# A branch for the general case: eight batches written out, or a loop over the batches with dynamic addresses

## The chip, the cores and the metric

One Trainium2 chip, one core of it. The metric is the device time in microseconds (us), the median of the runs of one program. The kernel before takes 548.6 us (three runs, 548.52 to 548.7).

## The reference

Eight batches of eight heads, 1024 positions of width 64. Keys and values are projected along the sequence to 64 rows (E and F), then comes softmax attention, and its output, laid out as 8192 tokens of width 512, goes through a gated feed-forward block of width 1536.

```python
k_proj = einsum('ks,bhsd->bhkd', E, k)
v_proj = einsum('ks,bhsd->bhkd', F, v)
scores = scale * matmul(q, k_proj.transpose(0, 1, 3, 2))
attn = exp(scores - max(scores))
attn = attn / (sum(attn) + 1e-09)
x = matmul(attn, v_proj)          # then (batch, seq, heads * width), 8192 x 512
g, val = x @ w_gate, x @ w_val
out = (g * sigmoid(g) * val) @ w_out
```

## The kernel before

The work is cut into 16 chunks `c` of 512 tokens, two to a batch, and each chunk into 12 slices `f` of the feed-forward width. The program has two halves.

**The main path** (lines 797 to 977) is one region written out by hand: `tc.manual_schedule()` keeps the instructions of each engine in the order in which they are written. A loop in Python over 192 steps (lines 966 to 975) emits `f_g` and `f_v`, eight matmuls of 128x512 with the tanh on ScalarE and two products on VectorE. Between them `run_slot` drops the attention of the next batches into numbered slots, and `late` gives the second matrix product of the chunk before (`f_m`: seven half-size products in place of eight, with sums on VectorE and GpSimd). Loads go out on GpSimd's queue, results on SyncE's. `f_m_last` (lines 671 to 710) ends the last chunk; its six last transfers of 128 KB go out from lines 695 and 706.

The main path takes the exponential without subtracting the row's maximum. Therefore it adds up the sums of the exponentials (`u_Z`, `u_sum`) and makes a flag from them (`u_flag`): 0 if the sum is sane, 1 if not. `u_bad` (lines 763 to 765) loads the flag into a register of each of the five engines and marks a place for a branch hint there, in slot 88 after 48 x 6 (the flag is loaded at 518.8 to 522.7 us of the span).

**The general path** (`general`, lines 767 to 795) is the other half. It stands behind `with tc.If(bad[0] != 0, label="general")` (line 979) and computes all again, with the maximum subtracted (`exp_maxed`, line 374: eight exponentials in place of one). In Python it is `for b in range(B)`: each of the eight batches is written out with constant addresses. An engine whose flag is 0 branches over all of it, to the code after the `If`, where the program ends: SyncE waits for every output transfer and every engine, a barrier of all engines follows, the semaphores are cleared, and a second barrier closes (in the trace these have line 1006, the branch and its arm line 979). The inputs of the measurement give a flag of 0: no instruction of `exp_maxed` stands in the trace.

The two halves share their helpers: `load_k`, `load_v`, `load_q`, `u_N`, `rows_of` and so on are called by both, and `maxed` tells them that it is the general path that is being emitted.

Of the kernel before, what the change touches and what calls it, by code (L numbers as in the profile page):

```python
# [15 lines left out]
B = 8  # L16
H = 8
S = 1024
# [5 lines left out]
NJ = S // P  # L24
# [3 lines left out]
CH = 2  # L28
# [11 lines left out]
def kernel(  # L40
# [55 lines left out]

    kb, vb, qb, xT, hT = {}, {}, {}, {}, {}

    def load_k(b, h0=0, h1=H):
        if b or maxed:  # L100
            kb[b] = kv_pool.tile([P, H, NJ, D], BF16, name="kb", tag="kb")
        nc.gpsimd.dma_start(
            out=kb[b][:, h0:h1].rearrange("p h j d -> p h (j d)"),
            in_=k[b, h0:h1].rearrange("h (p j) d -> p h (j d)", j=NJ),
        )

    def load_v(b, heads=(0, H)):
        if heads[0] == 0:
            vb[b] = kv_pool.tile([P, H, NJ, D], BF16, name="vb", tag="vb")
        t = vb[b]  # L110
        for h0, h1 in zip(heads, heads[1:]):
            nc.gpsimd.dma_start(  # L112
                out=t[:, h0:h1].rearrange("p h j d -> p h (j d)"),
                in_=v[b, h0:h1].rearrange("h (p j) d -> p h (j d)", j=NJ),
            )

    def load_q(b, ch, js=(0, 4), hs=(0, H)):
        if js[0] == 0 and hs[0] == 0:
            qb[b, ch] = q_pool.tile([P, H, 4, D], BF16, name="qb", tag="qb")
        js, hs = slice(*js), slice(*hs)  # L120
        nc.gpsimd.dma_start(  # L121
            out=qb[b, ch][:, hs, js, :].rearrange("p h j d -> p h (j d)"),
            in_=q[b, hs].rearrange("h (p c j) d -> p c h j d", c=2, j=4)[:, ch, :, js, :].rearrange(
                "p h j d -> p h (j d)"
            ),
        )
# [16 lines left out]
    maxed = []  # L143
# [14 lines left out]
    def u_KV(b, what="kv", hs=(0, H), at="a"):  # L158

        key = (b, what)  # L160
        if key not in kvp:
            kvp[key] = bank(at, [P, H, D], FP32, "kvp")
        t = kvp[key]
        h0, h1 = hs
        todo = [x for x in (("k", 0, ET, kb), ("v", 64, FT, vb)) if x[0] in what]
        for j in range(NJ):
            for _, lo, w, src in todo:
                nc.tensor.matmul(  # L168
                    out=t[lo : lo + 64, h0:h1].rearrange("p h d -> p (h d)"),
                    lhsT=w[:, j, :],  # L170
                    rhs=src[b][:, h0:h1, j, :],
                    start=(j == 0),
                    stop=(j == NJ - 1),
                )
        if "k" in what:
            nc.scalar.copy(out=ks[b % 2][0:64, h0:h1], in_=t[0:64, h0:h1])
        if "v" in what:
            tv = t[64:128].rearrange("p (g r e) d -> p g r e d", r=2, e=2)
            for r in range(2):
                vs = VS[b % 2][64 * r : 64 * r + 64].rearrange("p (g e) d -> p g e d", e=2)  # L180
                nc.vector.tensor_copy(out=vs, in_=tv[:, :, r])
        if h1 == H:
            kvp.pop(key)
# [76 lines left out]
    def u_KT(b, at="a", prs=(0, NPAIR)):  # L260

        t = bank(at, [P, NPAIR, KP], FP32, "kTp")
        for pr in range(*prs) if b > 1 or maxed else ():
            nc.tensor.matmul(
                out=t[:, pr, :],
                lhsT=ks[b % 2][:, 2 * pr : 2 * pr + 2, :].rearrange("p h d -> p (h d)"),
                rhs=ident_bf[:, 0:KP],  # L270
                start=True,
                stop=True,
            )
        for g in range(2) if b < 2 and not maxed else ():
            turn_ksp(t, b, g)
        bd = BD[b % 2][:].rearrange("p (a c) k -> p a c k", c=2)
        for c in range(2):
            src = t[64 * c : 64 * c + 64, slice(*prs)]
            nc.vector.tensor_copy(out=bd[0:64, slice(*prs), c, 0:64], in_=src)
            nc.vector.tensor_copy(out=bd[64:128, slice(*prs), c, 64:128], in_=src)  # L280
# [31 lines left out]
    def first_batch(kind, shape, name):  # L312

        n, ms = kept[kind]
        kept[kind] = (n + 1, ms)
        return hs_tile(ms[n % len(ms)], shape, name)

    def u_T(b, u, at="a", eng=nc.scalar):
        ch, w = divmod(u, 4)
        g, i = divmod(w, 2)  # L320
        ps = bank(at, [P, 4, P], BF16, "qTp")
        src = qb[b, ch]
        for n in range(4):
            nc.tensor.transpose(  # L324
                out=ps[:, n, :],
                in_=src[:, 4 * g + n, 2 * i : 2 * i + 2, :].rearrange("p j d -> p (j d)"),
                identity=ident_bf[:],
            )
        t = first_batch("q", [P, 4, P], "qT")
        copy(eng, t[:], ps[:])  # L330
        qT[b, u] = t
# [17 lines left out]
    def u_S(b, u, at="a"):  # L349
        ch, w = divmod(u, 4)  # L350
        g, i = divmod(w, 2)
        ps = bank(at, [P, 4, P], FP32, "sc")
        if (b, ch) in by_dma:
            t = qT[b, ch, "d"][:].rearrange("p (h i) t -> p i h t", i=2)[:, i, 4 * g : 4 * g + 4]
        else:
            t = qT.pop((b, u))
        for n in range(4):
            slot = (0, 2, 1, 3)[n] if (b, ch) in by_dma or maxed else n
            nc.tensor.matmul(  # L359
                out=ps[:, slot, :], lhsT=t[:, n, :], rhs=BD[b % 2][:, 4 * g + n, :], start=True, stop=True  # L360
            )
        e = aw.tile([P, 4, 2, KP], FP32, name="ee", tag="ee", bufs=4)
        ee[b, u] = e
        if maxed:
            exp_maxed(e, ps)
            return
        nc.scalar.activation(  # L367
            out=e[:].rearrange("p h j k -> p (h j k)"),
            in_=ps[:].rearrange("p a k -> p (a k)"),
            func=AF.Exp,  # L370
            scale=scale,
        )
# [20 lines left out]
    def u_N(b, u, eng=nc.gpsimd):  # L393
        ch, w = divmod(u, 4)
        g, i = divmod(w, 2)
        if (b, ch) in by_dma:
            if (b, ch, "d") not in AA:
                AA[b, ch, "d"] = aw.tile([P, 4, H, KP], BF16, name="AAd", tag="AAd")
            a = AA[b, ch, "d"][:, 2 * i : 2 * i + 2, 4 * g : 4 * g + 4, :]
        else:  # L400
            a = AA[b, u] = first_batch("a", [P, 2, 4, KP], "AA")
            a = a[:]
        zr, r = rr.pop((b, u))
        eng.tensor_tensor(  # L404
            out=a.rearrange("p j h k -> p h j k"),
            in0=ee.pop((b, u))[:],
            in1=r.unsqueeze(3).to_broadcast([P, 4, 2, KP]),
            op=ALU.mult,
        )
        unwatched.append(zr)  # L410
        if b or u > 3 or maxed:
            u_Z()

    unwatched = []
# [1 line left out]
    def u_Z():  # L416
        for zr in unwatched:
            nc.gpsimd.tensor_tensor(out=zsum[:], in0=zsum[:], in1=zr[:].rearrange("p i n -> p (i n)"), op=ALU.add)
        unwatched.clear()
# [142 lines left out]

    def rows_of(c):
        b, ch = divmod(c, CH)
        return out[b * S : (b + 1) * S, :].rearrange("(p c j) d -> p c j d", c=CH, j=4)[:, ch]

    def quarter(t, half, x):
        return t[:, HF * half : HF * (half + 1), HC * x : HC * (x + 1)]
# [12 lines left out]
    hs = {}  # L581
# [185 lines left out]
    def general():  # L767

        for d in (kb, vb, qb, xT, hT, kvp, qT, ee, rr, AA, AT, hs, xx, zz, tt, yo):
            d.clear()  # L770
        maxed.append(True)
        ring["wide"] = False
        by_dma.clear()
        for b in range(B):
            load_k(b)
            load_v(b)
            u_KV(b)
            u_KT(b)
            for ch in range(CH):
                c = CH * b + ch  # L780
                load_q(b, ch)
                for u in range(4 * ch, 4 * ch + 4):
                    u_T(b, u)
                    u_S(b, u)
                    u_R(b, u)
                    u_N(b, u)
                    u_A(b, u)
                u_PVt(b, ch, (0, 1), ("aa", "yz"))
                for f in range(NFT):
                    f_g(c, f)  # L790
                    f_v(c, f)
                for m in (1, 2, 5, 6, 7):
                    h_sum(c, m, 0, HF, nc.vector)
                for n in range(14):
                    f_m(c, n)

    with tc.manual_schedule():
# [3 lines left out]
        for i in range(2):  # L801
            nc.scalar.dma_start(
                out=kraw[i][:],
                in_=k[0, 2 * i : 2 * i + 2].rearrange("h (p j) d -> p h (j d)", j=NJ),
# [161 lines left out]
        for t in range(NIT):  # L966
            c, f = divmod(t, NFT)
# [9 lines left out]
        assert not slots and not late  # L977

    with tc.If(bad[0] != 0, label="general"):
        with tc.manual_schedule():  # L980
            general()

# [1 line left out]
_INS = ['q', 'k', 'v', 'E', 'F', 'moe_w_gate', 'moe_w_val', 'moe_w_out']  # L984
# [26 lines left out]
```

## Time and profile before

| what | value |
|---|---|
| median of three runs | 548.6 us |
| the profiled execution's own time | 548.97 us |
| its span, first to last instruction | 547.2 us |
| granted TensorE clock | 0.999 |
| TensorE matmul, busy | 537.9 us |
| VectorE, busy | 413.1 us |
| GpSimd, busy | 306.0 us |
| ScalarE, busy | 232.8 us |
| DMA, mean over the span | 115 GB/s |

The span holds all but 1.8 us of the profiled execution. "Busy" counts an engine's computing instructions; waits, branches and the issue of transfers are not in it, though each has a record with its line. The chain of waits follows the work that ended last back to its start. The packets of the two queues of the kind "instruction" are the engines' program code on its way to them.

### The profile page before, as it was taken

What the parts mean: (1) busy time and instruction counts of PE and PEld (TensorE: products, weight loads), DVE (VectorE), ACT (ScalarE), POOL (GpSimd) and SP (SyncE); (2) the same over time, 40 slices, a digit from 0 to 9 for tenths busy, and PEclk for the clock granted to TensorE, in tenths of its full rate; (3) what the DMA queues carried; (4) which work ended last, traced back from release to release, by engine and by line L of the source; (5) the groups of instructions that cost most, each with busy time, mean ns of one, the idle gap of its engine ahead of it and who ended that gap; (6) DMA issues with size and microseconds to landing.
All of it is one profiled execution on the core that took longest, in us unless ns stands there. A gap on an engine that the chain in (4) does not pass through costs nothing.

```text
span 547.2 us, 9546 instructions
## 1 busy us (share of the span) xinstructions
PE 537.9 (98%) x3558; PEld 313.8 (57%) x3558; DVE 413.1 (76%) x702; ACT 232.8 (43%) x416; POOL 306.0 (56%) x428
## 2 busy tenths in 40 slices
PE   8999999999999999999999999999999999999995
PEld 4654445556556555566555665566555655555664
DVE  3787897779578876779677795687857887675883
ACT  3564453354444434344434444434444443443331
POOL 6962495478616964087632966258651676416171
PEclk9999999999999999999999999999999999999999
DMA  9999969929921699009961199513992124101003
GB/s 196 191 196 195 165 146 189 178 78 162 196 67 41 103 200 197 31 11 153 197 151 39 40 152 206 106 40 65 172 199 67 39 78 78 40 38 40 17 23 120
DMA packets 112228, 62.93 MB, mean 115 GB/s; under 512 B 65968, under 2 KB 103856, under 8 KB 112176
## 3 DMA queue, kind: packets, MB, share of 16 engines
q0 software_dynamic: 43952, 29.49, 38.2%
q1 hardware_dynamic: 67392, 31.46, 26.5%
q10 hardware_dynamic: 832, 1.31, 0.8%
q8 instruction: 29, 0.48, 0.4%
q14 instruction: 23, 0.19, 0.1%
HBM read 60.29 MB, written 16.78 MB: 141 GB/s over the span
## 4 chain that ended last, share of the span: by engine, by line
PE 94%; DMA 2%; POOL 1%; ACT 0%; issue 0%; DVE 0%; POOLq 0%; DVEq 0%; ACTq 0%
PE vps L515 31%; PE gps L515 30%; PE yps L617 25%; PE sc L359 2%; DMA wv<-in_moe_w_val_dram 2%; PE kvp L168 2%; PE yps L551 2%; PE pv L461 1%; POOL vb L112 0%; POOL qb L121 0%; POOL AA L404 0%; PE kvp L207 0%; PE kvp L192 0%; PE qTp L324 0%; PE yps L515 0%
## 5 line engine op out<-in xcount | busy, mean ns | idle before, releaser
L527 ACT ACTIVATE th<-gps 128x512 f32<-128x512 f32 x191 | 114.1, 597 | 198.3 <-PE gps L515 196.1
L515 PE MATMUL vps<-xT,wv 128*128 128x512 bf16 (+1 forms) x776 | 197.6, 377 | 0.8 <-DMA wv<-in_moe_w_val_dram 0.7
L515 PE MATMUL gps<-xT,wg 128*128 128x512 bf16 (+1 forms) x772 | 196.5, 377 | 0.0
L534 DVE SCALAR_TENSOR_TENSOR s<-th,gps 128x512 f32<-128x512 f32 x191 | 129.3, 677 | 60.7 <-ACT th L527 59.5
L539 DVE SCALAR_TENSOR_TENSOR hT<-s,vps 128x512 bf16<-128x512 f32 x192 | 132.1, 688 | 21.7 <-PE vps L515 1.7
L600 POOL TENSOR_TENSOR hs<-hT 128x256 bf16<-128x256 bf16 x180 | 118.8, 683 | 47.2 <-DVE hT L539 46.7
L515 PEld LDWEIGHTS <-wv 128*128 128x128 bf16 x776 | 73.1, 98 | 85.4 <-issue 6.7
L617 PEld LDWEIGHTS <-hs 128*128 128x128 bf16 x900 | 88.1, 98 | 34.6 <-issue 0.6
L515 PEld LDWEIGHTS <-wg 128*128 128x128 bf16 x776 | 74.1, 98 | 51.4 <-issue 0.2
L647 POOL TENSOR_TENSOR tt<-tt,ysb 128x512 f32<-128x512 f32 x28 | 35.6, 1270 | 106.4 <-DVE tt L646 106.4
L404 POOL TENSOR_TENSOR AAd<-ee,zr 128x512 bf16<-128x512 f32 x56 | 58.4, 1044 | 30.1 <-ACT ee L367 17.6
L617 PE MATMUL yps<-ws,hs 128*128 128x256 bf16 x540 | 68.6, 273 | 0.2 <-DVE ysb L686 0.2
L367 ACT ACTIVATE ee<-sc 128x512 f32<-128x512 f32 x64 | 37.8, 595 | 31.6 <-PE sc L359 30.4
L617 PE MATMUL yps<-ws,hT 128*128 128x256 bf16 x360 | 48.8, 273 | 0.0
L617 PE MATMUL yps<-wo,hs 128*128 128x256 bf16 x360 | 48.6, 273 | 0.1
L636 POOL TENSOR_TENSOR tt<-xs 128x256 f32<-128x256 f32 x30 | 28.1, 937 | 36.7 <-ACT xs L634 36.0
L389 DVE TENSOR_REDUCE zr<-ee 128x8 f32<-128x512 f32 x64 | 43.3, 677 | 5.1 <-ACT ee L367 4.8
L600 DVE TENSOR_TENSOR hs<-hT 128x1536 bf16<-128x1536 bf16 (+1 forms) x49 | 45.2, 928 | 0.1
L617 PEld LDWEIGHTS <-hT 128*128 128x128 bf16 x360 | 35.2, 98 | 16.0
L634 ACT COPY xs<-yps 128x512 f32<-128x512 f32 x30 | 17.6, 586 | 28.0 <-PE yps L617 24.7
L641 ACT COPY ysb<-yps 128x512 f32<-128x512 f32 x30 | 17.6, 586 | 27.5 <-PE yps L617 27.5
L470 ACT CAST xT<-pv 128x512 bf16<-128x512 f32 x56 | 28.8, 599 | 0.0
(108 smaller groups left out, 324.8 us busy)
## 6 DMA issues: line engine op xcount, KB each, us to landing
out_dram<-ysb SPq DMA_DIRECT2D x27, 512.0 KB, 2.7
qb<-in_q_dram POOLq DMA_DIRECT2D x14, 512.0 KB, 18.1
kb<-in_k_dram POOLq DMA_DIRECT2D x7, 1024.0 KB, 10.8
vb<-in_v_dram POOLq DMA_DIRECT2D x7, 1024.0 KB, 15.8
wo<-in_moe_w_out_dram POOLq DMA_DIRECT2D x2, 768.0 KB, 21.6
out_dram<-ysb SPq DMA_DIRECT2D x6, 256.0 KB, 2.5
kraw<-in_k_dram ACTq DMA_DIRECT2D x2, 512.0 KB, 5.3
qb<-in_q_dram POOLq DMA_DIRECT2D x4, 256.0 KB, 8.2
```

What stands on the lines that cost most here:

```text
L367: nc.scalar.activation(out=e[:].rearrange("p h j k -> p (h j k)"), in_=ps[:].rearrange("p a k -> p (a k)"), func=AF.Exp, scale=scale,)
L389: nc.vector.reduce_sum(out=z, in_=e[:], axis=AX.X)
L404: eng.tensor_tensor(out=a.rearrange("p j h k -> p h j k"), in0=ee.pop((b, u))[:], in1=r.unsqueeze(3).to_broadcast([P, 4, 2, KP]), op=ALU.mult,
L470: nc.scalar.copy(out=xT[b, ch][:, kt, :], in_=ps[:])
L515: nc.tensor.matmul(out=ps[:, ts], lhsT=(wg, wv)[w][:, kt, f * P : (f + 1) * P], rhs=x[:, kt, ts], start=(kt == 0), stop=(kt == NKT - 1),)
L527: nc.scalar.activation(out=th[:], in_=ps[:], func=AF.Tanh, scale=0.5)
L534: nc.vector.scalar_tensor_tensor(out=s1[:], in0=th[:], scalar=1.0, in1=g[:], op0=ALU.add, op1=ALU.mult)
L539: nc.vector.scalar_tensor_tensor(out=hT[c][:, f, :], in0=s1[:], scalar=0.5, in1=ps[:], op0=ALU.mult, op1=ALU.mult)
L600: eng.tensor_tensor(out=hs[c, m][:, fs, :], in0=quarter(hT[c], *a)[:, fs], in1=quarter(hT[c], *b)[:, fs], op=op,)
L617: nc.tensor.matmul(out=ps, lhsT=lhsT, rhs=ws[m][:, f, :] if rhs is None else rhs, start=(start and f == 0), stop=(f == HF - 1), skip_group ...
L636: nc.gpsimd.tensor_tensor(out=t[:, 0], in0=xs[:, 0], in1=xs[:, 1], op=ALU.add)
L647: nc.gpsimd.tensor_tensor(out=t[:], in0=t[:], in1=yo[c, p][:, 1:3], op=ALU.subtract)
```

## The change

The Python loop of `general` becomes a loop of the program, `tc.For_i(0, B)`: its body is one batch, and the number of the batch is a register, `turn`. The addresses that depend on the batch (the loads of q, k, v and the rows of the output) are made from that register by a new helper, `batch`. While `turn_of` is empty, as it is when the main path is emitted, `batch` gives the same slice as before. `manual_schedule` moves from outside `general` to inside the loop. In the general path `u_N` no longer adds to the sums that the flag is made from (`u_Z`).

```diff
+    turn_of = []
+
+    def batch(t, b):
+        return t[bass.ds(turn_of[0], 1)].rearrange("o h s d -> (o h) s d") if turn_of else t[b]
+
     def load_k(b, h0=0, h1=H):
...
-            in_=k[b, h0:h1].rearrange("h (p j) d -> p h (j d)", j=NJ),
+            in_=batch(k, b)[h0:h1].rearrange("h (p j) d -> p h (j d)", j=NJ),
...
-                in_=v[b, h0:h1].rearrange("h (p j) d -> p h (j d)", j=NJ),
+                in_=batch(v, b)[h0:h1].rearrange("h (p j) d -> p h (j d)", j=NJ),
...
-            in_=q[b, hs].rearrange("h (p c j) d -> p c h j d", c=2, j=4)[:, ch, :, js, :].rearrange(
+            in_=batch(q, b)[hs].rearrange("h (p c j) d -> p c h j d", c=2, j=4)[:, ch, :, js, :].rearrange(
...
+        if maxed:
+            return
         unwatched.append(zr)
-        if b or u > 3 or maxed:
+        if b or u > 3:
             u_Z()
...
-        return out[b * S : (b + 1) * S, :].rearrange("(p c j) d -> p c j d", c=CH, j=4)[:, ch]
+        return batch(out.rearrange("(b h s) d -> b h s d", b=B, h=1), b)[0].rearrange("(p c j) d -> p c j d", c=CH, j=4)[:, ch]
...
-        for b in range(B):
+        with tc.For_i(0, B) as turn, tc.manual_schedule():
+            turn_of.append(turn)
+            b = 0
             load_k(b)
...
     with tc.If(bad[0] != 0, label="general"):
-        with tc.manual_schedule():
-            general()
+        general()
```

## The prediction

> **What bounds the kernel now.** I read the page's busy times first, then the chain of waits, then the rows of the branch (line 979) and of the code that ends the program (line 1006), then the DMA queues and the last output transfers.
>
> The busy times and the chain, from the page:
>
> ```profile
> PE 537.9 (98%) x3558; PEld 313.8 (57%) x3558; DVE 413.1 (76%) x702; ACT 232.8 (43%) x416; POOL 306.0 (56%) x428
> ...
> PE 94%; DMA 2%; POOL 1%; ACT 0%; issue 0%; DVE 0%; POOLq 0%; DVEq 0%; ACTq 0%
> ```
>
> TensorE is busy for 537.9 of 547.2 us and holds 94% of the chain. All of that is the main path: lines 374 to 382, which only the general path uses, have no row. So the branch is skipped, and what the change rewrites is not executed. It can touch the time in three places: the main path's own instructions, the jump over the general path, and the code after it. The busy time by stage shows how little is left for the last two:
>
> ```profile
> 500.00:538.00 38.00, 37.93 (x248) 24.09 (x247) 28.70 (x44) 11.79 (x20) 19.05 (x23) 1.00 0.11 42
> ...
> 541.00:544.00 3.00, 0.70 (x7) 0.39 (x4) 0.84 (x2) 0.00 (x0) 0.00 (x0) 1.00 0.81 275
> 544.00:547.20 3.20, 0.00 (x0) 0.00 (x0) 0.00 (x0) 0.00 (x0) 0.00 (x0) 0.85 0.07 17
> ```
>
> The columns are window, length, busy PE, PEld, DVE, ACT, POOL, clock, DMA share, GB/s. TensorE has hardly a gap until 538 (37.93 of 38 us) and ends at 541.7; from 544 on nothing computes and hardly a byte moves. The tail of 5.4 us is jump, landing of the outputs, and closing barriers. The rows of the jump:
>
> ```profile
> L979 POOLq EVENT_SEMAPHORE  x5: 17/43/43, 539.2 to 539.5; - x5
> L979 POOLq COMPARE_BRANCH  x1: 59/59/59, 536.6 to 536.6; - x1
> L979 POOLq INC_SWDGE_SEM  x1: 500/500/500, 539.6 to 539.6; - x1
> L979 PEldq COMPARE_BRANCH  x1: 652/652/652, 540.6 to 540.6; - x1
> L979 PEldq EVENT_SEMAPHORE  x1: 51/51/51, 541.7 to 541.7; - x1
> L979 DVEq COMPARE_BRANCH  x1: 84/84/84, 541.8 to 541.8; - x1
> L979 SPq COMPARE_BRANCH  x1: 74/74/74, 542.3 to 542.3; - x1
> L979 DVEq EVENT_SEMAPHORE  x1: 21/21/21, 542.4 to 542.4; - x1
> L979 ACTq COMPARE_BRANCH  x1: 68/68/68, 542.9 to 542.9; - x1
> L979 ACTq EVENT_SEMAPHORE  x1: 17/17/17, 545.9 to 545.9; - x1
> ```
>
> Each engine has a branch and, on the other side, a semaphore instruction. GpSimd loses 2.5 us between the two (536.7 to 539.2) and ScalarE 2.9 (542.96 to 545.89); VectorE and TensorE lose nothing that their own last work doesn't explain. The queues that carry code:
>
> ```profile
> q8 instruction: 29, 0.48, 0.4%
> q14 instruction: 23, 0.19, 0.1%
> ```
>
> The trace's packets put times to them: TensorE's code comes in 16 KB packets (q8), the other engines' in 8 KB (q14), about one for every 128 instructions that an engine has executed. Around the jump they start at 537.63 (GpSimd's target, between its two rows), 538.42, 539.81, 543.09 (16 KB, 0.99 us), 543.43, 543.56 (8 KB, 0.65 us) and 546.49. So a jump to code that is not there costs its engine 2.5 to 2.9 us. The hints explain who pays: VectorE and TensorE fetch another packet after theirs (523.1 and 520.3) and before the branch, GpSimd and ScalarE don't.
>
> What ends the span is a third thing, the outputs:
>
> ```profile
> L706 SPq DMA_DIRECT2D out_dram<-ysb x2: 401/413/425, 541.3 to 541.8; - x2
> ...
> DMA to landing us min/median/max: 2.0/4.0/4.2
> ```
>
> Each transfer reports 16 times, once per DMA engine. Normally the 16 lie within 0.1 to 0.3 us; of the last four 13 to 15 do (by 544.04), the rest come 2.35 to 2.55 us after the first, the last at 546.18. Between them lie the code packets of 543.09 to 544.21. SyncE goes on at 546.20, and barrier, clearing and second barrier end at 547.16.
>
> **The change part by part.** On the scale of the profiled execution: 547.2 us of span and 1.8 around it, 548.97. The median of the runs is 0.37 lower.
>
> 1. *Main path.* With `turn_of` empty, `batch(t, b)` is `t[b]`; `k[b][h0:h1]` is the slice `k[b, h0:h1]`, and the regrouped `out` has the same rows and strides. `u_N` keeps `u_Z` there. The order is written by hand. The same 9546 instructions, the same waits: 0. Below and above, if a wait or an SBUF place shifts after all: 0.1% of the busy TensorE, 0.5 us either way.
>
> 2. *Flag and hints.* Same place, same instructions: 0.
>
> 3. *GpSimd's jump.* One batch in its general path has 8 loads and stores, 8 `u_N` and 8 sums in `m_34` and `m_16`, 24 instructions where 8 x 32 stood (with `u_Z`); with waits, register work and the loop I estimate 50 to 120. GpSimd's packets came at its instructions 65, 195, 319 and 452, so the next piece begins near 580 and the branch stands at 553: the target, near 603 to 673, lies in the piece already there. The 2.5 us go, and are worth 0: GpSimd ended its first DRAIN at 541.4 and waits until SyncE's 546.3. Without that cover they would cost what they cost now.
>
> 4. *ScalarE's jump.* One batch is 64 exponentials, 24 tanh and 25 copies, 113 instructions, and some 40 waits, so over 150 with the loop. Its packets came at 70, 195, 321, 450 and 577; the branch, its 704th, is at the very end of a piece, and the target some 170 further lies beyond the next piece. The 2.9 us stay: 0. If the target were near enough, ScalarE would be through at 543.1, and the last landing (546.18) would still hold SyncE: a gain of 0.02 us at most.
>
> The Trainium skill ("Runtime: NRT & Kernel Launch", section "Instruction fetch mechanics") says that code is kept in blocks of 16 KiB, 256 instructions, two at a time, fetched in sequence, and that a taken branch out of them stalls. The stall is in the rows; the block is not, for ScalarE, whose 8 KB packets come every 128 instructions. By the page's block ScalarE's target would be in the window and its stall would go; the sum would be the same, for the landing is late anyhow.
>
> 5. *TensorE and VectorE.* One batch is 492 matmuls and as many weight loads, and 112 VectorE instructions, both with waits on top. TensorE's target stays outside what it holds; VectorE's is fetched by hint now. Same hint, same packets, and after the jump the next piece in sequence (543.09, 543.43): 0.
>
> 6. *The arm that skips.* Now it holds one semaphore instruction an engine (17 to 51 ns) and on GpSimd five and the 500 ns of INC_SWDGE_SEM, which set the counts to what the general path would have left. Fewer or other counts: 0 to -0.5 us of GpSimd, hidden as in 3. What a loop asks of this arm no row shows. Below: nothing. Above: a barrier of its own, by the nearest rows, those that end the program: 0.9 us from SyncE's DRAIN (546.27) to the end, and 0.8 for SyncE's twelve waits, 60 to 70 ns each: 1.7. I take 0, because the counts before and after the loop are known when the program is built, as they are now.
>
> 7. *Code packets against the last outputs.* By 3 to 5 the packets after 543 stay. Below: all of them gone, outputs land at 544.04 in place of 546.18: -2.1. Above: one more in the same place, 1 us by the 16 KB packet. I take 0.
>
> 8. *Clearing.* 178 ns now; with more semaphores for the loop, up to the same again: 0 to +0.2. I take 0.
>
> Sum: 548.97 + 0 = 548.97, less 0.37: **548.6 us**. Own range 548.0 to 549.3.
>
> **The rivals.**
>
> *The loop costs on the skipping side (slower).* A loop of the program must put its semaphores back between turns; if both arms must then meet at the same counts, the arm that skips resets too, with all engines stopped. Price 1.7 us (step 6), place after line 979: 550.3. It decides as soon as that arm holds a DRAIN and a barrier. For it: the profile's one reset has a barrier on each side. Against: today's arm gets by with additions.
>
> *The code after the jump falls badly in its piece (slower).* ScalarE's landing place moves. If the end of a piece comes within the few instructions of the barrier, a second fetch follows the first: 0.6 us to the packet (545.89 to 546.49), 0.5 for it, 1.2 to go on (GpSimd: 538.02 to 539.19), so 2.3: 550.9. For it: about 8 places of 128.
>
> *The fetches leave the outputs alone (faster).* With a short general path fewer engines need far code. If neither ScalarE nor TensorE fetched between 542 and 544.2, the outputs would land 2.1 us earlier: 546.5. Against: step 4 and 5, and the packet after the jump, which comes even on a hit.
>
> *The change doesn't stay out of the main path.* The helpers are shared; a moved wait would give 548.1 to 549.1.
>
> **How the numbers follow.** The bound between "same" and the rest is 0.2%, 1.1 us, about what a measurement of this kernel can tell from no change. Forecast 0.70 (same). Loop costs 0.13, bad place 0.05 (both slower). Fetches gone 0.09 (faster). Main path touched 0.03, a third each way. Faster 0.10, same 0.71, slower 0.19. The range goes up to the first rival's 550.3, so that only the second and the upper part of the first are left out, and down to 547.4, which leaves out the full 2.1 us: about 0.2 outside.
>
> **What would show it.** Right: the same count of instructions up to the branch and TensorE's end at 541.7; GpSimd's two rows close together; ScalarE's still 2.9 us apart; a last landing 2 us after the others. Wrong: a DRAIN or a clearing between branch and end (first rival), a packet of code late in the last 2 us with an engine standing still (second), or landings within 0.3 us and SyncE free by 544.3 (third).

## The result and the profile after

The kernel after takes 548.25 us (median of 22 runs, 547.85 to 549.05); the kernel before, beside it, 548.88 us (median of 22). The ratio is 0.9984, 95% interval [0.9977, 0.9992]: 0.16% faster, small but outside its interval. Two repeats (e2 and e18 below, on two chips) gave 0.9979 [0.9966, 0.9993] and 0.9979 [0.9968, 0.9991]. The forecast was no change. So the question is a small one: where do 0.6 to 1.2 us come from, in a program that executes almost the same instructions?

The profiled execution of the kernel after took 548.89 us, with a span of 547.2 us. It is one of the slower of its runs, and within 0.1 us of the one of before; the pair of traces alone does not show the gain. From the page after:

```profile
span 547.2 us, 9550 instructions
...
PE 536.7 (98%) x3558; PEld 313.6 (57%) x3558; DVE 413.7 (76%) x702; ACT 232.8 (43%) x416; POOL 305.9 (56%) x428
...
q8 instruction: 29, 0.48, 0.4%
q14 instruction: 22, 0.18, 0.1%
...
PE 94%; DMA 4%; ACT 0%; issue 0%; DVE 0%; POOL 0%; DVEq 0%; ACTq 0%; POOLq 0%
```

The computing instructions are the same in number on every engine. One 8 KB packet of code is gone from q14, and there are four more instructions (9550, not 9546). Those four stand in the rows of the entry code (line 1003), on GpSimd's sequencer:

```profile
L1003 POOLq MOVE  x4: 29/29/35, 0.2 to 0.4; - x4
```

They stand in every trace with the loop and in none without it, and hold the start back: the first matmul begins at 1.43 us in place of 1.19.

The rows of the branch, now line 988:

```profile
L988 POOLq EVENT_SEMAPHORE  x5: 17/43/43, 537.8 to 538.2; - x5
L988 POOLq COMPARE_BRANCH  x1: 59/59/59, 537.0 to 537.0; - x1
...
L988 ACTq COMPARE_BRANCH  x1: 68/68/68, 543.3 to 543.3; - x1
L988 ACTq EVENT_SEMAPHORE  x1: 17/17/17, 546.2 to 546.2; - x1
```

GpSimd now goes on 0.8 us after its branch (2.5 before); ScalarE still stands for 2.9 us. The last outputs, first in the view of line 713 (after), then in SyncE's waits from 538 us on (after):

```profile
DMA to landing us min/median/max: 1.9/3.7/3.9
```

```profile
SPq L1014 <- DMA out_dram<-ysb: 2.7, 3, 2.3
```

Of the last four transfers one lands after 1.9 us, most after 3.7 to 3.9 (before: 2.0, and 4.0 to 4.2). SyncE waits up to 2.3 us for them, and the span ends 1.0 us after the last of them.

To see where a difference lies, I cut each trace at two instructions that all kernels share: the **start**, up to the beginning of the 21st tanh of the feed-forward (`th`); the **main part**, from there to the beginning of VectorE's last product; and the **tail**, the rest of the span. The main part takes 473.50 us in every trace of this study but one (the one that adds work to it). So a change that doesn't touch the main path acts on the start or the tail.

| traces (one execution each) | start | main | tail |
|---|---|---|---|
| before | 68.24 | 473.50 | 5.42 |
| after, and its two repeats | 68.62, 68.34, 68.38 | 473.50 | 5.12, 5.00, 4.96 |

The starts after include the 0.24 us of the four moves. In after and its repeats the device time has less outside the span: time less span is 1.57 to 1.63 us in the mean of their runs, 1.84 to 1.87 in those of before, so most of the 0.24 us doesn't reach the device time there. That the moves are the reason is not shown: e4 below has the same moves, and 1.81.

### The profile page after: what moved, and what is told of

Read it like the earlier page. It is cut to its first block, busy times and chain, and to the rows that moved or that the text cites. A ratio compares the mean times of both kernels' runs of the same rounds, so it can differ in the third digit from the quotient of the medians.

```text
span 547.2 us, 9550 instructions
## 1 busy us (share of the span) xinstructions
PE 536.7 (98%) x3558; PEld 313.6 (57%) x3558; DVE 413.7 (76%) x702; ACT 232.8 (43%) x416; POOL 305.9 (56%) x428
## 4 chain that ended last, share of the span: by engine, by line
PE 94%; DMA 4%; ACT 0%; issue 0%; DVE 0%; POOL 0%; DVEq 0%; ACTq 0%; POOLq 0%
PE vps L522 31%; PE gps L522 30%; PE yps L624 25%; PE sc L364 2%; DMA wv<-in_moe_w_val_dram 2%; PE kvp L173 2%; PE yps L558 2%; PE pv L468 1%; DMA qb<-in_q_dram 1%; POOL AA L409 0%; PE kvp L212 0%; PE kvp L197 0%; PE qTp L329 0%; PE pv L448 0%; PE yps L522 0%
```

## The experiments

All ratios are to the kernel before on the same chip, in the same rounds. "Start" and "tail" are those of the table above; the "first cast" is when VectorE begins its first cast of k, which ends its wait for the first load (`kraw`).

### First four: is it the loop, the moves, or the length?

e1 is a copy of before and e2 a copy of after. The other two take the two sides of the change apart. e3 keeps the Python loop and constant addresses but writes out one batch:

```diff
-        for b in range(B):
+        for b in range(1):
```

e4 has the loop of the program, with all eight batches written out in its body:

```diff
         with tc.For_i(0, B) as turn, tc.manual_schedule():
             turn_of.append(turn)
-            b = 0
+            for b in range(B):
```

> The kernel before once more, unchanged, to see how far two loads of one program differ. If the gain of the change (ratio 0.9984) is a property of the programs, this stands at 1.0000 +- 0.0008 against the kernel before, and its trace has the tail of 5.7 us from the start of the last matmul to the end, with GpSimd 2.5 us between its branch and the next instruction. If the gain is only where a program happens to lie in memory or which run is looked at, this differs from the kernel before by as much as the changed kernel does, 0.15%.

> The changed kernel once more. Property of the program: ratio 0.998 to 0.999, start (matmul number 100) 0.24 us later by the four register moves, unless the start's loads make up for it, tail 0.3 us shorter. Chance of placement: any ratio from 0.998 to 1.002.

> The kernel before with only the first of the eight batches in the general path, constant addresses, no loop (the general path, which is not executed here, would compute one batch alone). The code that is jumped over is as short as in the change, but the four register moves at the start are not there. Theory A, the short jump in the tail is the gain: as fast as the changed kernel or 0.24 us faster, 547.9 to 548.3, tail 5.4 us. Theory B, the gain comes from what the moves do to the start (loads fall differently): as the kernel before, 548.6 to 548.9.

> The changed kernel with all eight batches written out in the loop's body: loop, dynamic addresses and the four register moves at the start as in the change, but a jump as long as before. Theory A (short jump): as the kernel before or 0.24 us slower, 548.6 to 549.1, GpSimd's 2.5 us back, tail 5.7 us. Theory B (start): as the changed kernel, ratio 0.9984.

Measured: e1 1.0008 [0.9999, 1.0016]; e2 0.9979 [0.9966, 0.9993]; e3 0.9977 [0.9968, 0.9987]; e4 1.0003 [0.9991, 1.0015]. The two short programs are 0.2% faster, with the loop or without it; the two of eight batches are not, with the loop or without it. So neither the loop, nor the dynamic addresses, nor the four moves move the time by more than these intervals. What the gain goes with is how many batches are written out in the skipped code. (e1 lies at the edge of what was expected of a copy, so 0.1% is about what the same program can differ by.)

### Second four: which effect of the length?

e6 writes out four batches (`range(4)`); e7 emits `general()` twice, sixteen batches. e8 has one batch, and 340 additions on GpSimd behind it in the general path, so that GpSimd alone has far to jump:

```diff
             general()
+            for _ in range(340):
+                nc.gpsimd.tensor_tensor(out=zsum[:], in0=zsum[:], in1=zsum[:], op=ALU.add)
```

e5 leaves out `u_bad`, the `If` and the general path: it has no jump at all.

> No general path at all: the If, what it holds, and the loading of the flag with its hints are left out (the sums and the flag itself are still computed). No jump, and the shortest code. If code fetched at the jump is what delays the last outputs, they land within 0.3 us of each other here and the tail is some 2 us shorter than in the short kernels: 546.0 to 546.5. If the start gains from short programs, its first load of k (512 KB) lands at 4.6 us as in the short kernels, not at 5.2 to 6.2.

> The kernel before with four of the eight batches in the general path, which is not executed (it would compute half). Theory 1, the far jump of GpSimd (its target is 200 instructions away, not in the piece it holds) costs the time: as the kernel before, ratio 1.000. Theory 2, the length of the whole program acts on the first loads: half way, ratio 0.9988 +- 0.0005. Theory 3, it is a matter of where things lie in memory: anywhere between 0.997 and 1.002.

> The kernel before with the general path written out twice, not executed. Theory 1 (GpSimd's far jump): as the kernel before, 1.000. Theory 2 (length of the program): slower by as much again, ratio 1.002 to 1.003, first load of k later still. Theory 3 (place in memory): anywhere.

> One batch in the general path as in the kernel with the short static one, plus 340 additions on GpSimd behind it (the general path would spoil its sums; it is not executed): GpSimd jumps as far as before, the other engines as in the short kernel, and the program is only 22 KB longer. Theory 1 (GpSimd's far jump): as the kernel before, 1.000, GpSimd 2.5 us between its branch and the next instruction. Theory 2 (length of the program): as the short kernel, 0.9977, though GpSimd stands still 2.5 us.

Measured: e6 0.9978 [0.9969, 0.9987]; e7 0.9987 [0.9978, 0.9996]; e8 0.9979 [0.997, 0.9988]; e5 0.9937 [0.9924, 0.9951].

**GpSimd's jump is not the gain.** In e8 its stall is back, and the kernel is as fast as after (line 979 of e8):

```profile
L979 POOLq EVENT_SEMAPHORE  x5: 17/43/43, 538.7 to 539.0; - x5
L979 POOLq COMPARE_BRANCH  x1: 59/59/59, 536.1 to 536.1; - x1
```

The two are 2.6 us apart and cost nothing. In e6 it is the same (536.5 and 539.0).

**"The longer, the slower" falls too:** sixteen batches are faster than eight, and four are not half way between one and eight (0.9988 was expected for that) but as fast as one.

**e5 prices the jump.** Its last outputs, line 706:

```profile
DMA to landing us min/median/max: 1.8/1.9/2.0
```

and SyncE's wait for them from 538 us on:

```profile
SPq L1003 <- DMA out_dram<-ysb: 1.3, 4, 0.4
```

With no jump no packet of code starts between 538.3 and 545 us, all last transfers land within 2.0 us, and SyncE's longest wait is 0.4 us in place of 2.3. From the last matmul's start to the end of the span it takes 3.65 us (4.9 to 5.7 in the traces with a jump): 1.3 to 2.1 us is what the jump costs in these traces, inside the 2.1 that the prediction gave as the bound of its step 7. In device time e5 takes 2.0 us less than e6 and e8, run beside it (546.46 against 548.43 and 548.45 us). e5 leaves out the loading of the flag and the hints too; its main part is 473.50 us all the same.

### Third four: around eight, and ScalarE's stall

e9 writes out seven batches, e10 eight and then four more. e12 is before with a 1 MB tensor more in device memory, used only in the general path. e11 is after, with 20 small copies on ScalarE right behind the branch hint:

```diff
         tc.mark_branch_hint_location("general", hint=bad[0], engines=tuple(ENG))
+        for _ in range(20):
+            nc.scalar.copy(out=sane[:, 0:1], in_=sane[:, 1:2])
```

> The kernel before with seven of the eight batches in the general path (the eighth is left out of it; the measured path is whole). Length theory with a threshold (code short enough is free, eight batches are too long): seven lies just under eight, so 0.9995 to 1.001 of before, first load of k landing over 5.5 us before VectorE casts it. Place theory (the length only moves where the code and the tensors lie, and eight batches happen to lie badly): nothing ties seven to eight; as fast as one, four and the loop, 0.9975 to 0.9985, the k cast at 4.6 to 5.0 us. Noise theory (no kernel differs): 1.000 within 0.001.

> The general path written out for eight batches and then for four more (never executed here). Length theory with a threshold: 1.000 to 1.001 of before, or slower still. Place theory: any value between 0.9975 and 1.001, decided by the start alone: the main path between the 21st tanh and VectorE's last product takes 473.5 us again, and the difference of the spans is that of the start within 0.5 us. Noise theory: 1.000.

> The changed kernel with 20 copies of 128x1 on ScalarE right after the branch hint, so that ScalarE enters its next piece of code between hint and branch (its branch is the 724th instruction in place of the 704th). Hint theory: an engine that enters a new piece after the hint fetches the target with it; ScalarE's 2.9 us between its two rows of the branch fall below 0.5 us. Then, by the theory that the late landing holds the end (step 4 of the prediction), the time changes by less than 0.3 us from the changed kernel's; by the rival that ScalarE's packets are what delays the landings, the last landing comes within 0.5 us of the first and the time falls by 1.5 to 2 us, to 0.994 to 0.996 of before. If the hint theory is wrong, the 2.9 us stay and the time with them.

> The kernel before with a tensor of 1 MB more in device memory and one transfer to it at the end of the general path (never executed), the code as long as before. Place theory, if tensors and code share the memory in an order that this tensor shifts: the start changes, the time 0.997 to 0.9995 of before or also slower. Length theory: 1.000 within 0.001, as the code is as long. No change would not decide against the place theory, as the tensor may lie apart.

Measured: e9 0.9987 [0.9975, 0.9999]; e10 0.9985 [0.9975, 0.9995]; e12 0.9996 [0.9984, 1.0008]; e11 1.0009 [0.9998, 1.002].

e9 and e10 lie between the short programs and eight batches. Their intervals leave out 1.000 (e9's only just) and hold 0.998: no threshold at eight, no rise beyond. Two expectations were missed: e9's first cast (5.14 us) lies between those of its two theories, and e10's span is 0.66 us shorter than before's with a start 0.16 us longer, so the start alone did not decide it; its tail is 4.60 us. e12 is inconclusive, as its expectation allowed.

e11 removes ScalarE's stall. Its branch, line 990:

```profile
L990 ACTq COMPARE_BRANCH  x1: 68/68/68, 544.4 to 544.4; - x1
L990 ACTq EVENT_SEMAPHORE  x1: 17/17/17, 544.8 to 544.8; - x1
```

ScalarE's 2.9 us are 0.48 now. The packets go with it: one of 8 KB starts at 525.2 us, between ScalarE's hint (523.4) and its branch (544.4), where the trace of after has none, and the last packet of after (546.8), behind ScalarE's branch, is gone. That the hint did this is not shown by e11 alone: with ScalarE past the edge of a piece, and the target by the prediction's estimate some 170 instructions on, the next piece in sequence could hold it as well. VectorE speaks for the hint: it has a packet between hint and branch in before (530.8 us, VectorE's by the count of its instructions), and goes on 0.5 us after its branch in every trace, over one batch or sixteen. No run leaves the hint out.

But the last transfers are as late as without the copies (line 713 of e11):

```profile
DMA to landing us min/median/max: 2.0/3.8/3.9
```

The tail is 5.19 us: taking away ScalarE's stall gains nothing. The kernel is 0.003 of before slower than the repeats of after, some 1.65 us (1.0009 less 0.9979, of 549.9), and that is the main part: the 20 copies (busy ACT 236.3 us in place of 232.8) lengthen it from 473.50 to 475.15 us, which the expectation (within 0.3 us of after) had not reckoned with.

### Last six: the first loads

By now the records pointed to the start. The first load of k is issued at the same moment in all these programs (0.7 us; 1.0 with the moves), but lands later in the long ones. The same two lines, the first casts and the time from issue to landing of the two first loads of k, of before, of e1 (the same program), and of e3 (one batch):

```profile
L156 DVE CAST kb<-kraw x4: 352/422/426, 5.3 to 7.8; 128x512 bf16<-128x512 f32 x3, 128x256 bf16<-128x256 f32 x1
...
DMA to landing us min/median/max: 4.5/5.3/6.2
```

```profile
L156 DVE CAST kb<-kraw x4: 286/427/719, 6.3 to 8.7; 128x512 bf16<-128x512 f32 x3, 128x256 bf16<-128x256 f32 x1
...
DMA to landing us min/median/max: 5.5/6.3/7.1
```

```profile
L156 DVE CAST kb<-kraw x4: 285/417/616, 4.6 to 7.4; 128x512 bf16<-128x512 f32 x3, 128x256 bf16<-128x256 f32 x1
...
DMA to landing us min/median/max: 3.9/4.8/5.8
```

The first of the two loads takes 4.5 and 5.5 us in the program of eight batches, 3.9 in that of one. What that can cost is seen in TensorE's waits in the first 12 us of e1, and of e3 in the same view:

```profile
PE efp L824 <- DMA Eraw<-in_E_dram: 1.5, 1, 1.5
PE warm L836 <- DVE zeros L814: 1.2, 1, 1.2
```

```profile
PE warm L836 <- DVE zeros L814: 1.2, 1, 1.2
PE sc L359 <- DVE BD L156: 0.7, 1, 0.7
```

In e1 the warm-up matmuls end before E has landed, TensorE stands for 1.5 us, and then its clock falls to a half for 3.4 us. The stretches of e1 (window, length, busy PE, clock, DMA share, GB/s):

```profile
8.00:10.00 2.00, 2.00 (x9) 0.51 1.52 198
10.00:12.00 2.00, 1.96 (x16) 0.64 1.39 195
```

In e3 it doesn't wait for E. A short wait for E does no such harm: the kernel after has one of 0.8 us and keeps its clock (1.00 in all stretches from 0 to 14 us), and so do e2 and e8 with 0.7. The one other trace that loses the clock is e12, eight batches too, after 1.3 us; the waits of e12 and of after in the same view:

```profile
PE efp L824 <- DMA Eraw<-in_E_dram: 1.3, 1, 1.3
```

```profile
PE efp L833 <- DMA Eraw<-in_E_dram: 0.8, 1, 0.8
```

E lands at 7.2 us in e1 and 7.1 in e12, and at 5.7 to 6.7 in every other trace with undelayed loads.

The single runs fit this. Of the 150 runs of before in this study 88 took more than 549.36 us; of the 89 runs of the seven series with one or four batches (after, e2, e3, e6, e8, e15, e18) none did. For 128 of the runs of before the mean granted clock is on record: all 20 with 0.996 or less, which is what e1's and e12's traces have, took 549.93 us or more; of the 89 only one has such a clock. So part of the gain is that runs which lose the clock early become rare; the traces of the pair itself, before and after, both keep it, and do not show the gain.

The same ordering over all programs:

| batches written out | ratio | first cast (us) | start (us) |
|---|---|---|---|
| none, no jump (e5) | 0.9937 | 4.48 | 67.91 |
| 1 (e3, e15; e8 with GpSimd's additions) | 0.9977, 0.9978; 0.9979 | 4.65, 4.77; 4.61 | 67.95, 67.96; 67.73 |
| 1 in the loop (after, e2, e18) | 0.9984, 0.9979, 0.9979 | 4.66, 4.99, 5.09 | 68.62, 68.34, 68.38 |
| 4 (e6) | 0.9978 | 4.73 | 68.06 |
| 7 (e9) | 0.9987 | 5.14 | 68.08 |
| 12 (e10) | 0.9985 | 4.99 | 68.40 |
| 16 (e7) | 0.9987 | 5.29 | 68.30 |
| 8 (before; e1, its copy) | 1; 1.0008 | 5.27; 6.25 | 68.24; 69.81 |
| 8 in the loop (e4) | 1.0003 | 5.74 | 68.90 |
| 8, spare tensor (e12) | 0.9996 | 5.96 | 69.43 |

(Casts and starts of the programs with the loop include the 0.24 us of the moves.) Where the cast is early the program is fast; where it is latest, slow. Each cast and start is from one execution, so a single row proves little, and the middle rows do not line up (e7 casts as late as before and is faster); what speaks is the order of the outer groups.

The last runs put the first loads off, to see whether they are slow because the program has just begun: six memsets on GpSimd, which the first loads wait for, in the program of eight batches (e13, e16) and in that of one (e14, e17).

```diff
+        for t in (kraw[0], kraw[1], kraw[0], kraw[1], ef[0], zeros):
+            nc.gpsimd.memset(t[:], 0.0)
         for i in range(2):
             nc.scalar.dma_start(
                 out=kraw[i][:],
```

> The kernel before with six memsets on GpSimd (four of 128x1024, one of 64x1024, one of 128x512) ahead of the first loads, which wait for them, so that all loads start about 5 us after the program has begun; general path of eight batches. To be set against the next run, the same with one batch. If the slower start of the long program comes from what is still under way when the program begins (code being brought in, say), the delay covers it, and the two agree within 0.0008; both are then slower than before by the delay. If it comes from where code and tensors lie, the first loads are as slow after the delay as without it: this run takes about 1.2 us (0.0022) more than the next.

> The same six memsets ahead of the first loads, with one batch in the general path (seven of eight left out of it). By the theory that something is still under way at the beginning: equal to the run before it within 0.0008. By the theory of the place: 0.0022 faster than it, and the first load of k on its way 0.5 us or more shorter.

> One batch written out in the general path (seven left out), loads not delayed: the control for the next two, on their chip. 0.9977 of before as in its first run; if it is within 0.0008 of before, this chip doesn't show the effect, and the two delayed runs decide nothing here.

> Eight batches, first loads delayed by six memsets, once more. If something still under way at the beginning slows the first loads, the delay covers it: within 0.0008 of the next run, while the control beside them is 0.002 below before. By the theory of the place: 0.002 above the next run.

> One batch, first loads delayed by six memsets, once more: equal to the run before within 0.0008 by the theory of something under way at the beginning; 0.002 below it by the theory of the place.

> The changed kernel once more, on the chip of the control: 0.998 of before, and within 0.001 of the control of one batch, if the effect of the change is that of the short code. If the effect depends on the chip, both move together towards 1.000.

Measured: e13 1.0074 [1.006, 1.0088] and e14 1.0068 [1.0054, 1.0081]; then, with the control on their chip, e15 0.9978 [0.9968, 0.9988], e16 1.0074 [1.0053, 1.0096], e17 1.0067 [1.0048, 1.0085], e18 0.9979 [0.9968, 0.9991]. The control takes 1.55 us off before (548.20 against 549.75 us); the delayed pairs differ by 0.09 and 0.13 us in their medians, and by 0.20 us in the mean of 11 runs each, standard error 0.33. So **with the loads delayed, the length of the skipped code costs nothing that can be measured**. (The weight lies on e16 and e17: beside e13 and e14 there was no control, and before itself took only 548.95 us there.)

That looks like the theory of something still under way at the beginning, but the traces leave it open. First, one of the delayed loads is still slower in the long program: the first cast is at 7.39 and 7.25 us (e13, e16) against 6.85 and 6.80 (e14, e17), 0.4 to 0.6 later, with the same memsets ahead. The second load of k and the load of E are not slower there (4.9 and 5.1 us from issue to landing against 5.3 and 6.4; 5.1 and 5.4 against 5.3 and 5.5). Second, the delay took the loads off the path. TensorE's waits in the first 12 us of e17:

```profile
PE warm L838 <- DVE zeros L816: 6.1, 1, 6.1
```

No load is in that list, nor in those of e14 and e16; only e13 has 0.4 us for E. The warm-up matmuls, which now begin at 6.1, last until after E has landed, and hide how late the first loads are. So these runs don't tell the two theories apart. They fit that the length acts through the first loads, since it costs nothing where the warm-up matmuls cover them; that nothing else at the beginning is involved they do not show.

## Why the prediction was wrong

**Step 1 failed: "main path ... the same 9546 instructions, the same waits: 0".** The instructions are the same (but for four moves, which the step missed; they put 0.24 us into the start of the span, and by e3 against e2 and e4 against e1 nothing measurable into the time), and the 473.50 us of the main part agree to the last digit. But it took equal instructions for equal time, and the start of the main path is not only instructions: it waits for loads from memory, and the first of them lands earlier in programs with little skipped code (first cast at 4.6 to 5.1 us against 5.3 to 6.3). The term was 0 with bounds of 0.5 us either way. The kernel as a whole fell by 0.63 us, by 0.97 and 1.17 in its repeats, and the starts of the traces put the term at about -1.0: the seven traces of one or four batches (e3, e6, e8, e15, after, e2 and e18, the last three less their 0.24) have a mean of 68.05, the four of eight (before, e1, e4 less 0.24 and e12) one of 69.03. Of this, 0.6 hang on e1 and e12, the two whose clock fell; before and e4 alone have 68.45. The prediction had looked for a moved wait in the program; that the length of code which nothing executes is itself a change did not occur to it as a term, and it was none of its rivals. The fourth rival has the right place, a moved wait in the main path, and 548.1 us at its lower end, at a chance of 0.03; but its cause, the shared helpers, is not the one. That the measured 548.25 us lies near the forecast 548.6 is luck: before, run beside it, took 548.88, and the sum had no term that takes anything off.

**Step 7 stands within what single traces tell.** It took 0, with bounds of -2.1 and +1. The tails of the same traces have means of 4.93 and 5.19 us, but the groups overlap (4.61 to 5.12, and 4.93 to 5.42). Its lower bound was right: e5, with no packets of code beside the last outputs, saves 1.3 to 2.1 us there. (Of the reports of the last four transfers of before, 14 or 15 of 16 come early, not 13 to 15; nothing in the sum hangs on it.) The rival built on it (546.5) did not come: in the kernel after, packets still run from 543.28 to 544.74, and three of the last four transfers land about 2 us late.

**Steps 2 to 6 and 8 were right.** GpSimd's stall went and was worth nothing; e6 and e8 bring it back at no cost. ScalarE's stayed, and e11, which removes it, has no shorter tail. VectorE and TensorE fetch as before. The arm that skips holds the same 14 instructions and no barrier, so the main rival (550.3) falls; the clearing takes 177 ns, not 178. The second rival (a second packet with an engine standing still) did not come either.

On the Trainium skill's page "Runtime: NRT & Kernel Launch", section "Instruction fetch mechanics", the prediction set blocks of 256 instructions against 8 KB packets of 128 on ScalarE. e11 agrees with the packets: 20 instructions more carried ScalarE over the edge which the prediction had counted out (its 705th instruction), and the stall went; by an estimate from the page's blocks of 256 its target would have been in reach in the kernel after, where it still stalls.

**What stays open** is why the first loads land later. That the order doesn't follow the length (one and four batches early; seven, twelve and sixteen later; eight latest) and the 0.5 us that remain on one load after a delay speak for where code and tensors lie in memory. That the other delayed loads are not slower speaks for something still under way at the beginning. No run shows an address, and e12 did not move the time outside its interval. So it is shown that the gain goes with how much code is written out in the skipped arm, and by the traces that the start has it; why the loads land later stays open. Open too is how much of it is the clock: runs of before spread over 548.3 to 552.3 us, those of e15 over 548.0 to 549.0, and each run has one trace.

## What to carry to other kernels

An arm that is never taken is not free: here the time fell by 0.2% when one or four batches stood in it in place of eight, without a rule that more code costs more, and the jump over it costs 1.3 to 2.1 us at the end, where packets of code run beside the last outputs. When two programs execute the same instructions, cut their traces at shared instructions: the part that agrees to the last digit is out of the question, and the start, which waits for memory, is the first place to look. A test that delays or removes something must be read for what became the bound in its place; here the warm-up matmuls did.

## What the runs showed of the hardware

- From the end of the branch to the next instruction a jump to far code cost ScalarE 2.4 to 3.1 us and GpSimd 2.5 to 2.8. ScalarE, which enters no further piece of its code between hint and branch, stood for 2.8 us in after, and for 0.4 where it does (e11); VectorE, which does, stood for 0.5 in every trace.
- With packets of code beside the last small output transfers, one or two of the 16 parts of a transfer came 2.0 to 2.6 us after its first (before and after); without a jump (e5) all 16 came within 0.2 us. That these parts share DMA engines with the code is not shown.
- The same 512 KB load, issued at the same 0.7 us, took 3.9 to 4.0 us to land with one or four batches of unexecuted code in the program, 4.5 to 5.5 with eight, and 4.2 to 4.5 with seven, twelve and sixteen.
- A gap of 1.5 us in TensorE's work at 6 to 8 us (e1), and one of 1.3 (e12), was followed by 3.4 us at half the clock; gaps of 0.7 and 0.8 at the same place (e2, e8, after) were not.
